# Scaling the next pair's keys behind the row-sum addition on GpSimd, and the first pair's loads split over two queues

## Chip, cores and metric

The kernel runs on one core of one Trainium2 chip. The metric is the device time of one execution in microseconds (us). Before the change it is 1041.75 us, the median of three runs (1041.70 to 1041.97). The profile discussed here is one profiled execution with a span of 1039.9 us, in which TensorE was granted 0.993 of its full clock.

## What is computed

Thresholded attention over 8 batches and 8 heads (sequence 576, head size 64), and then a mixture of experts in which a hash of the token number picks one of 8 experts:

```python
scores = scale * np.matmul(q, k.transpose(0, 1, 3, 2))
thresh = np.max(scores, axis=-1, keepdims=True) - tau
scores = np.where(scores >= thresh, scores, -1000000000.0)
scores = scores - np.max(scores, axis=-1, keepdims=True)
attn = np.exp(scores)
attn = attn / (np.sum(attn, axis=-1, keepdims=True) + 1e-09)
attn_out = np.matmul(attn, v)
# x = attn_out as (B*S, H*D)
expert_idx = token_ids * np.int64(2654435761) % np.int64(E)
for e in range(E):
    xe = x[expert_idx == e]
    out[expert_idx == e] = np.maximum(xe @ w1[e], 0.0) @ w2[e]
```

All data is float32. The host lays q and k out with the head size ahead of the sequence (`qT`, `kT`), which is done before the launch and is not part of the time.

## The kernel before, in words

**Two stages.** The attention takes the first 484 us or so, the experts the rest. The change lies in the attention stage and in its start.

**Pairs and steps.** Attention works on pairs: two heads of one batch, 32 pairs in all, numbered `p`. A pair is cut into five steps `s`. Step 0 holds the last 64 queries of both heads (128 rows), steps 1 to 4 hold 128 queries each, once for each head (`j` = 0, 1). So a pair has nine score tiles of 128 x 576. The main loop runs over `n = 5*p + s`, and the order of instructions in each engine's queue is the order in which the loop's body emits them (`tc.manual_schedule()`); the framework adds only the semaphore waits.

**One score tile.** TensorE makes the scores from `q_sb` and the scaled `k_sb` (`score`, L201), two 288-wide halves into two banks of PSUM. VectorE negates them into `ns` and takes their minimum (`negate`, L212). GpSimd adds the threshold constant to that minimum (`thr`, L219, a 128 x 2 operation). ScalarE takes the exponential (`expo`, L226) into `w`. One step later VectorE masks: `w = (ns <= thr) * w`, with the row sum as accumulator (`mask`, L237; it reads two tiles, `ns` and `w`, both in SBUF). TensorE then transposes `w` (`turn_w`, L248), ScalarE copies the transposes out (`put_wT`, L264 and L269), and TensorE multiplies by v (`av_part`, L279).

**Finishing a pair.** The last masks of pair `q` are emitted in step 0 of the next pair. In step 1 GpSimd adds 1e-9 to the nine row sums (`add_eps`, two tiny operations at L309); they wait for the last mask of pair `q`. In step 2 VectorE takes the reciprocal (L603), which waits for `add_eps`. In step 0 of the pair after that, VectorE multiplies the transposed output by it (`put_xm`, L318).

**Keys.** `load_pair(p + 2)` loads keys and queries two pairs ahead, at step 0, all on the SyncE queue. Keys come in three pieces (L163, L164, L165), queries in two of 288 KB (L167). `scale_k(p + 1)` (L181) multiplies the next pair's keys by 1/8 and by the `keep_any` flag, in place, in one GpSimd operation over 128 x 576. Before the change it is emitted at the top of step 1, so that GpSimd takes it ahead of that step's `add_eps`:

```python
if s == 1 and p + 1 < NP:
    scale_k(p + 1)
...
if s == 1 and 0 <= q < NP:
    add_eps(q)
```

**The routing of tokens.** In between, VectorE does the small integer work of the routing. It is a generator, `route()`, cut into pieces by bare `yield` lines. The loop takes one piece at step 3 (at its top) and one at step 0 (behind `negate`, ahead of `put_xm`). As the generator is cut before the change, nearly all heavier pieces (the 128 x 288 operations L366, L374, L408, L412, L415 and the like) fall into step 0 and the light ones into step 3; the piece at L381 to L388, which contains two small matmuls in between, falls into step 3. Once slots are known, 36 scatters on GpSimd (L464) are spread over pairs 12 to 20, four to a pair, none of them in step 1. Ten row gathers (L101) are emitted in pairs 26 and 27, one at each step.

**The start.** The first pair's queries are issued on the ScalarE queue, its keys on SyncE behind the 512-byte load of tau; then follow the token numbers, v and the second pair. GpSimd scales the whole first k tile, then writes its constants (iota, masks, memsets), then takes `thr` of step 0, and then `scale_k(1)`.

Of the kernel before, what the change touches and what calls it, by code (L numbers as in the profile page):

```python
# [14 lines left out]
ALU = mybir.AluOpType  # L15
# [5 lines left out]
def kernel(  # L21
# [12 lines left out]
    nc = tc.nc  # L34

    B, H, D, S = qT.shape
    N, DIN = out.shape
    E, _, F = w1.shape
    P = 128
    HP = H // 2  # L40
    NP = B * HP
# [3 lines left out]
    SCALE = 1.0 / float(D) ** 0.5  # L45
    assert D == 64 and S == 4 * P + 64 and SCALE == 0.125 and E == 8
    S2 = S // 2
    NQ = 4
    TAIL = NQ * P
# [38 lines left out]
    keep_any = consts.tile([P, 1], FP32, name="keep_any")  # L88
# [32 lines left out]
    with tc.tile_pool(name="a_q", bufs=1) as a_q, \  # L121
# [26 lines left out]
        av = ps_av.tile([P, 2, 512], FP32, name="av")  # L148
        kts, rss, recs, scs, nss, stats, ws = {}, {}, {}, {}, {}, {}, {}

        def load_pair(p, q_engine=nc.sync):
            hp, b = divmod(p, B)
            h0 = 2 * hp
            q_sb = q_bufs[p % 3]
            k_sb = a_k.tile([P, 2, S2], FP32, name="k_sb")
            kts[p] = k_sb


            def keys(c0, shift, width):
                ap = [[S, D], [D * S + shift, 2], [1, width]]  # L160
                return bass.AP(tensor=kT.tensor, offset=(b * H + h0) * D * S + c0, ap=ap)

            nc.sync.dma_start(out=k_sb[0:64, :, 64:S2], in_=keys(64, -64, S2 - 64))  # L163
            nc.sync.dma_start(out=k_sb[0:64, :, 0:64], in_=keys(0, TAIL, 64))  # L164
            nc.sync.dma_start(out=k_sb[64:P], in_=keys(S2, -64, S2))  # L165
            for r in range(2):
                q_engine.dma_start(out=q_sb[64 * r:64 * r + 64],  # L167
                                   in_=qT[b, h0:h0 + 2].rearrange("h d s -> d h s"))

        def load_v(p):  # L170
            hp, b = divmod(p, B)
# [8 lines left out]
        def scale_k(p):  # L180
            nc.gpsimd.tensor_scalar(out=kts[p][:], in0=kts[p][:], scalar1=keep_any[:],  # L181
                                    scalar2=SCALE, op0=ALU.mult, op1=ALU.mult)
# [121 lines left out]
        def add_eps(p):  # L304

            rec = a_st.tile([P, 2 * NS], FP32, name="rec")
            rs = rss.pop(p)
            for i, cols in ((0, 9), (9, 1)):
                nc.gpsimd.tensor_scalar(out=rec[:, i:i + cols], in0=rs[:, i - i // 9:i - i // 9 + cols],  # L309
                                        scalar1=1e-9, scalar2=None, op0=ALU.add)  # L310
            recs[p] = rec
# [20 lines left out]
        def route():  # L332
# [22 lines left out]
            nc.gpsimd.memset(keep[:, :, 0:1], 0.0)  # L355
            nc.gpsimd.memset(ones_e[:], 1.0)
            yield

            nc.vector.tensor_scalar(out=eid[:], in0=tid32[:, :, 0], scalar1=E - 1, scalar2=None,
                                    op0=ALU.bitwise_and)
# [4 lines left out]
                                    in0=eidf[:, None, :].to_broadcast([P, E, NTC]),  # L367
# [3 lines left out]
            for e in (0, E // 2):  # L371
# [6 lines left out]
                if e == 0:  # L378
# [14 lines left out]
                                    scalar2=float(P - 1), op0=ALU.add, op1=ALU.max)  # L393
            nc.vector.tensor_scalar(out=ot_i[:], in0=ot_i[:], scalar1=7, scalar2=None,
                                    op0=ALU.logical_shift_right)
# [4 lines left out]
                                         op1=ALU.add)  # L400
# [19 lines left out]
                                    scalar2=None, op0=ALU.bitwise_and)  # L420
            nc.vector.tensor_scalar(out=rank_i[:, 2], in0=rank_i[:, 0], scalar1=13, scalar2=None,
                                    op0=ALU.logical_shift_right)
# [5 lines left out]
                                    op0=ALU.mult)  # L428
            yield
            nc.vector.tensor_scalar(out=ovt[:], in0=ovt[:], scalar1=float(P),  # L430
                                    scalar2=float((E - 1) * CAP), op0=ALU.mult, op1=ALU.add)
# [8 lines left out]
                                           op0=ALU.add, op1=ALU.add)  # L440
# [6 lines left out]
                out=oc, in0=iota_f[:, 0:NOV, None].to_broadcast([P, NOV, E]),  # L447
# [6 lines left out]
                                    scalar1=float(E - 1), scalar2=None, op0=ALU.min)  # L454
# [6 lines left out]
        def scatters():  # L461
# [13 lines left out]
            for _ in range(4):  # L475
# [2 lines left out]

        nc.sync.dma_start(out=tau_in[:],
                          in_=bass.AP(tensor=tau.tensor, offset=0, ap=[[0, P], [1, 1]]))  # L480
        load_pair(0, nc.scalar)
        nc.sync.dma_start(out=tid32[:],
                          in_=bass.AP(tensor=dataclasses.replace(token_ids.tensor,
                                                                 shape=[2 * N], dtype=I32),
# [8 lines left out]
                                op0=ALU.is_ge)  # L493
# [8 lines left out]
            nc.vector.memset(v_sb[64:P, 4, 0:64], 0.0)  # L502
        nc.vector.memset(oT[:, 0:64], 0.0)
        nc.vector.memset(xg_bufs[0][:], 0.0)

        def constants():

# [64 lines left out]
        with tc.manual_schedule():  # L572

            tr = ps_tr.tile([P, 2, 512], FP32, name="tr")
            for _ in range(18):
                nc.tensor.transpose(tr[:, 0, 0:P], ident[:], ident[:])
            scale_k(0)
            constants()
            next(pieces)
            score(0, 0)  # L580
            for n in range(LAST + NS + 1):
                p, s = divmod(n, NS)
                m = n - 2
                if s == 0 and p + 2 < NP:
                    load_pair(p + 2)
                if s == 0 and p + 1 < NP:
                    load_v(p + 1)
                if s == 1 and p + 1 < NP:
                    scale_k(p + 1)
                if s == 2 and p in (20, 24):  # L590
                    load_w1(p // 4 - 5)
                if s == 2 and p in (22, 26):
                    load_w2((p - 22) // 4)

                if s == 3 and n < LAST:
                    next(pieces, None)
                if s == 1 and 3 <= p < 2 + len(xg_bufs):
                    nc.sync.dma_start(out=xg_bufs[p - 2][:], in_=xg_bufs[0][:])
                q = p - 1
                if s == 1 and 0 <= q < NP:  # L600
                    add_eps(q)
                if s == 2 and 0 <= q < NP:
                    nc.vector.reciprocal(recs[q][:], recs[q][:])  # L603
                if n == LAST:
                    tr = ps_sc.tile([P, 2, 512], FP32, name="sc")
                    early_xT(tr, 0, 2, 0, CO - 1)
                if s == 0 and p >= 2:
                    turn_o()
                if n == LAST:
                    tr = ps_sc.tile([P, 2, 512], FP32, name="sc")  # L610
                    early_xT(tr, 2, 4, 0, CO - 1)
                if s in (1, 2) and 0 <= q < NP and n != LAST + 1:
                    av_part(q, 0, ((0, 1, 2), (3, 4))[s - 1])
                if n < LAST and s in (1, 2):
                    negate(n, 0)
                    expo(n, 0)
                if s == 2 and 0 <= q < NP:
                    put_oT(0)
                if n > LAST:
                    fill(1)  # L620
                turned = 0 <= m < LAST
                if turned:
                    tr = turn_w(m, 0)
                    put_wT(m, 0, tr)
                if n == LAST:
                    tr = ps_sc.tile([P, 2, 512], FP32, name="sc")
                    early_xT(tr, 4, 5, 0, CO - 1)
                    put_xm(p - 2)
                    av_part(q, 0, (0, 1, 2))
                if n >= LAST:  # L630
                    fill(1)
                if s in (3, 4) and 0 <= q < NP:
                    av_part(q, 1, ((0, 1, 2), (3, 4))[s - 3])
                if n < LAST and s not in (1, 2):
                    negate(n, 0)
                    expo(n, 0)
                if s == 0 and n < LAST:
                    next(pieces, None)
                if s == 0 and p >= 2 and n != LAST:
                    put_xm(p - 2)  # L640
                if s == 4 and 0 <= q < NP:
                    put_oT(1)
                if s in (3, 4) and turned:
                    tr = turn_w(m, 1)
                if n + 1 < LAST:
                    score(n + 1, 0)
                if s == 4 and turned:
                    put_wT(m, 1, tr)
                if n < LAST and heads(n) == 2:
                    negate(n, 1)  # L650
                    expo(n, 1)
                if s == 3 and turned:
                    put_wT(m, 1, tr)
                if n + 1 < LAST:
                    score(n + 1, 1)
                if s in (0, 1) and turned:
                    tr = turn_w(m, 1)
                    put_wT(m, 1, tr)
                if 0 < n <= LAST:
                    for j in range(heads(n - 1)):  # L660
                        mask(n - 1, j)
                if s != 1 and placed:
                    next(scatter_pieces, None)


                g = n - G0
                if 0 <= g < 2 * KT:
                    fetch(g // KT, g % KT, 0)
                if n == LAST:
                    fill(1)  # L670
            for g in range(2 * KT):
                fetch(g // KT, g % KT, 1)
            fill(FO * 2 * (CO - 1) - 18)
            tr = ps_tr.tile([P, 2, 512], FP32, name="tr")
            early_xT(tr, 0, KT, CO - 1, CO)
            fill(18)
            late_h()
# [123 lines left out]
```

## Time and profile before

| stretch of the span, us | TensorE busy | VectorE busy | ScalarE busy | GpSimd busy |
|---|---|---|---|---|
| 0 to 11 | 5.54 | 2.71 | 1.28 | 3.09 |
| 11 to 26 | 12.66 | 14.58 | 11.49 | 5.77 |
| 180 to 310 | 127.92 | 128.82 | 111.94 | 87.90 |
| 456 to 484 | 26.55 | 15.76 | 14.27 | 4.20 |
| 484 to 1040 | 545.54 | 56.28 | 48.92 | 109.24 |

The table is the view of busy time by stretches. A busy time close to the length of its stretch says that the engine hardly ever stood still there. In the expert stage that is TensorE alone; in the attention TensorE and VectorE are both close to it. TensorE's ends are modelled, so a busy TensorE is not proof that it works at its peak. The share of VectorE over the whole span, 49%, is an average over the two stages and says nothing of either.

### The profile page before, as it was taken

To read this page: it belongs to the slowest core of one execution; us is meant where nothing else is said; L and a number is where in the kernel's file an instruction comes from. 1 tells how busy PE (TensorE), PEld (TensorE's weight loads), DVE (VectorE), ACT (ScalarE), POOL (GpSimd) and SP (SyncE) were. 2 spreads that over 40 slices of the span, in tenths; PEclk is the share of its full clock that TensorE was granted. 3 is DMA by queue.
4 is the path that set the end of the run, shared out by engine and by line. 5 is a ranking of instruction groups with operands and counts; after the bars stand their busy time and mean duration, and the time that the engine had idled before them with its cause. 6 is when DMAs were issued, how large, how long until landed. Compare 5 with 4: busy or idle time off the path is not lost. (4 is left out here: it accounts for less than half of the span.)

```text
span 1039.9 us, 19768 instructions
## 1 busy us (share of the span) xinstructions
PE 1017.7 (98%) x7432; PEld 613.6 (59%) x7432; DVE 514.3 (49%) x1352; ACT 445.8 (43%) x725; POOL 315.6 (30%) x431
## 2 busy tenths in 40 slices
PE   6999999999999999999999999999999999999996
PEld 4666666656666666666547557466475574664752
DVE  6999999999999999992300101001001010010000
ACT  4888888888898888891201000000010000000100
POOL 3233332667762246232514022140140221001001
PEclk8999999999999999999999999999999999999998
DMA  7355544445464869301404231242042312200000
GB/s 163 80 127 135 126 118 111 102 116 115 101 178 111 258 139 245 82 25 28 136 36 135 100 104 56 106 141 84 33 135 100 105 54 104 98 5 32 10 18 28
DMA packets 91732, 103.46 MB, mean 99 GB/s; under 512 B 24301, under 2 KB 65391, under 8 KB 91636
## 3 DMA queue, kind: packets, MB, share of 16 engines
q1 hardware_dynamic: 83156, 82.68, 29.6%
q0 software_dynamic: 8192, 18.91, 5.3%
q8 instruction: 60, 0.98, 0.4%
q10 hardware_dynamic: 288, 0.59, 0.2%
q14 instruction: 36, 0.29, 0.1%
HBM read 81.87 MB, written 20.01 MB: 98 GB/s over the span
## 5 line engine op out<-in xcount | busy, mean ns | idle before, releaser
L717 PE MATMUL o_ps<-w_sb,h 128*122 128x512 f32 x640 | 280.6, 592 | 0.0
L226 ACT ACTIVATE w<-ns,nmx 128x576 f32<-128x576 f32 x288 | 220.3, 776 | 48.5 <-DVE ns L212 48.5
L703 PE MATMUL sc<-xT,w_sb 128*128 128x305 f32 x896 | 231.2, 419 | 0.0
L237 DVE SCALAR_TENSOR_TENSOR w<-ns,thr,w 128x576 f32<-128x576 f32 x288 | 230.3, 831 | 0.0
L212 DVE TENSOR_SCALAR_CACHE_REDUCE ns<-sc 128x576 f32<-128x576 f32 x288 | 205.8, 746 | 10.1 <-PE sc L201 9.4
L703 PEld LDWEIGHTS sc<-xT,w_sb 128*128 128x128 f32 x896 | 169.1, 189 | 63.4 <-issue 3.4
L717 PEld LDWEIGHTS o_ps<-w_sb,h 128*122 128x122 f32 x640 | 115.5, 185 | 138.9 <-issue 138.5
L201 PE MATMUL sc<-k_sb,q 64*128 64x288 f32 (+1 forms) x1280 | 183.8, 430 | 6.2 <-DMA v<-in_v_dram 3.9
L721 POOL DMA_INDIRECT out_dram<-o,gidx x40 | 39.6, 989 | 414.0 <-ACT o L720 400.4
L219 POOL TENSOR_SCALAR thr<-nmx,drop 128x2 f32<-128x2 f32 (+1 forms) x160 | 98.8, 617 | 206.5 <-DVE ns L212 197.2
L248 PEld LDWEIGHTS tr<-ident,w 64*128 64x128 f32 x2624 | 106.8, 139 | 87.8 <-ACT wT_b L269 27.0
L711 DVE TENSOR_SCALAR h<-sc 128x610 f32<-128x610 f32 x28 | 22.2, 793 | 256.9 <-PE sc L703 256.9
L720 ACT COPY o<-o_ps 122x512 f32<-122x512 f32 x40 | 23.4, 586 | 293.4 <-PE o_ps L717 293.4
L248 PE MATMUL tr<-ident,w 64*128 64x64 f32 x2624 | 139.1, 230 | 2.5 <-ACT wT_a L269 2.0
L696 DVE COPY xT<-xT_ps 128x488 f32<-128x488 f32 x35 | 23.3, 665 | 183.4 <-PE xT_ps L694 183.4
L201 PEld LDWEIGHTS sc<-k_sb,q 64*128 64x128 f32 (+1 forms) x1280 | 93.1, 178 | 33.2 <-DVE ns L212 15.5
L279 PE MATMUL av<-wT_a,v 128*64 128x320 f32 (+1 forms) x704 | 100.4, 418 | 0.2 <-DVE xm L318 0.2
L709 ACT ACTIVATE h<-sc 128x610 f32<-128x610 f32 x28 | 19.0, 680 | 182.7 <-PE sc L703 182.7
L269 ACT COPY wT_a<-tr 128x512 f32<-128x512 f32 (+1 forms) x128 | 81.8, 639 | 20.2 <-PE tr L248 20.1
L269 ACT COPY wT_b<-tr 128x512 f32<-128x512 f32 (+1 forms) x128 | 81.2, 634 | 6.3 <-PE tr L248 3.8
L279 PE MATMUL av<-wT_b,v 128*64 128x256 f32 x640 | 83.2, 389 | 0.0
L279 PEld LDWEIGHTS av<-wT_a,v 128*64 128x64 f32 x704 | 43.7, 136 | 28.9 <-DVE xm L318 0.3
(97 smaller groups left out, 517.1 us busy)
## 6 DMA issues: line engine op xcount, KB each, us to landing
w_sb<-in_moe_w_dram SPq DMA_DIRECT2D x16, 2048.0 KB
q<-in_q_dram SPq DMA_DIRECT2D x62, 288.0 KB
v<-in_v_dram SPq DMA_DIRECT2D x32, 256.0 KB
xa_scratch<-xm SPq DMA_DIRECT2D x24, 256.0 KB
k_sb<-in_k_dram SPq DMA_DIRECT2D x32, 144.0 KB
k_sb<-in_k_dram SPq DMA_DIRECT2D x32, 112.0 KB
xg<-xg SPq DMA_DIRECT2D x9, 256.0 KB
xb_scratch<-xm SPq DMA_DIRECT2D x8, 256.0 KB
```

The costliest lines, as they stand in the source:

```text
L201: nc.tensor.matmul(sc[out_rows, i, 0:S2], lhsT=q_sb[rows, h, q0:q1], rhs=k_sb[rows, h], start=True, stop=True)
L212: nc.vector.tensor_scalar(out=ns[:].rearrange("p (i s) -> p i s", i=2), in0=sc[:, :, 0:S2], scalar1=-1.0, scalar2=None, op0=ALU.mult, op1= ...
L219: nc.gpsimd.tensor_scalar(out=thr[:, 0:j + 1], in0=stats[n][0][:, 0:j + 1], scalar1=drop[:], scalar2=None, op0=ALU.add)
L226: nc.scalar.activation(w, nss[n, j][:], AF.Exp, bias=stats[n][0][:, j:j + 1], scale=-1.0)
L237: nc.vector.scalar_tensor_tensor(out=w, in0=nss.pop((n, j))[:], scalar=stats[n][1][:, j:j + 1], in1=w, op0=ALU.is_le, op1=ALU.mult, accum_ ...
L248: nc.tensor.transpose(dst[:, r, 64 * c:64 * c + 64], src[rows, c0:c0 + P], ident[rows, rows])
L269: nc.scalar.copy(dst, tr[:, :, 0:64 * n_c].rearrange("p r (c q) -> p r c q", c=n_c))
L279: nc.tensor.matmul(av[64 * j:64 * j + 64, g, c0:c1], lhsT=v_sb[:, c, 64 * j:64 * j + 64], rhs=wT[g][:, i, c0:c1], start=(c == 0), stop=stop)
L703: nc.tensor.matmul(h_ps[:, i, 0:width], lhsT=w1_sb[:, co, fo * P:fo * P + P], rhs=xT[:, co, i * width:i * width + width], start=(co == 0), ...
L717: nc.tensor.matmul(o_ps[0:rows], lhsT=h_sb[:, fo, kt * rows:kt * rows + rows], rhs=w2_sb[:, fo, :], start=(fo == 0), stop=(fo == FO - 1))
L720: nc.scalar.copy(o_sb[0:rows], o_ps[0:rows])
L721: nc.gpsimd.indirect_dma_start(out=out[:, :], out_offset=bass.IndirectOffsetOnAxis(ap=idx, axis=0), in_=o_sb[:], in_offset=None, bounds_ch ...
```

## The change: what it does and what it is for

It has three parts.

1. `scale_k(p + 1)` is emitted behind `add_eps(q)` in step 1, not at the top of the step. On GpSimd the row-sum additions of the finished pair come first, and the scaling of the next pair's keys follows. It is meant to keep the long scaling from standing ahead of the additions, and from running beside the masks.
2. The first pair's loads are reordered: the third key piece goes to the ScalarE queue, at its head; behind it come the last 64 columns of the queries, which are all that step 0 needs. The other 512 columns follow on SyncE behind the other two key pieces. The first k tile is scaled by two engines, one head by VectorE and one by GpSimd, at once.
3. `route()` gets one more `yield` behind its memsets, so that each later piece comes half a turn later: what was taken at step 0 is now taken at step 3, and the other way round.

```diff
-        def load_pair(p, q_engine=nc.sync):
+        def load_pair(p):
...
+            def queries(engine, r, c0, c1):
+                engine.dma_start(out=q_sb[64 * r:64 * r + 64, :, c0:c1],
+                                 in_=qT[b, h0:h0 + 2, :, c0:c1].rearrange("h d s -> d h s"))
+
             nc.sync.dma_start(out=k_sb[0:64, :, 64:S2], in_=keys(64, -64, S2 - 64))
             nc.sync.dma_start(out=k_sb[0:64, :, 0:64], in_=keys(0, TAIL, 64))
-            nc.sync.dma_start(out=k_sb[64:P], in_=keys(S2, -64, S2))
+            (nc.sync if p else nc.scalar).dma_start(out=k_sb[64:P], in_=keys(S2, -64, S2))
+            if p:
+                for r in range(2):
+                    queries(nc.sync, r, 0, S)
+                return
+
             for r in range(2):
-                q_engine.dma_start(out=q_sb[64 * r:64 * r + 64],
-                                   in_=qT[b, h0:h0 + 2].rearrange("h d s -> d h s"))
+                queries(nc.scalar, r, TAIL, S)
+            for r in range(2):
+                queries(nc.sync, r, 0, TAIL)
...
             nc.gpsimd.memset(ones_e[:], 1.0)
             yield
+            yield
...
-        load_pair(0, nc.scalar)
+        load_pair(0)
...
+        for j, engine in enumerate((nc.vector, nc.gpsimd)):
+            engine.tensor_scalar(out=kts[0][:, j], in0=kts[0][:, j], scalar1=keep_any[:],
+                                 scalar2=SCALE, op0=ALU.mult, op1=ALU.mult)
...
-            scale_k(0)
             constants()
...
-                if s == 1 and p + 1 < NP:
-                    scale_k(p + 1)
...
                 if s == 1 and 0 <= q < NP:
                     add_eps(q)
+                if s == 1 and p + 1 < NP:
+                    scale_k(p + 1)
```

## The prediction, made before the changed kernel was run

> **What bounds the kernel.** I began with busy time by engine on the page and by stretch:
>
> ```profile
> PE 1017.7 (98%) x7432; PEld 613.6 (59%) x7432; DVE 514.3 (49%) x1352; ACT 445.8 (43%) x725; POOL 315.6 (30%) x431
> 26.00:180.00 154.00, 153.57 (x1868) 95.40 (x1868) 151.88 (x433) 131.96 (x216) 47.11 (x86) 1.00 0.47 116
> 310.00:456.00 146.00, 145.96 (x1786) 91.21 (x1782) 144.27 (x391) 125.90 (x206) 58.28 (x95) 1.00 0.61 154
> ```
>
> In the last two rows, the columns after the length are busy TensorE, its weight loads, VectorE, ScalarE, GpSimd. TensorE and VectorE both fill the attention. TensorE's ends are modelled, so the timeline must say which one waits. In an ordinary pair (VectorE and GpSimd lines only; start, duration):
>
> ```profile
> 423.33 0.82 DVE L318 TENSOR_TENSOR xm<-av,rec 128x640 f32<-128x640 f32 x1
> 423.58 0.30 POOL L219 TENSOR_SCALAR thr<-nmx,drop 128x1 f32<-128x1 f32 x1 [1.50 <-DVE ns L212]
> 423.85 0.75 POOL L181 TENSOR_SCALAR k_sb<-k_sb,keep_any 128x576 f32<-128x576 f32 x1
> 424.06 1.14 DVE L237 SCALAR_TENSOR_TENSOR w<-ns,thr,w 128x576 f32<-128x576 f32 x1
> ...
> 426.04 0.54 POOL L309 TENSOR_SCALAR rec<-rs 128x9 f32<-128x9 f32 x2 [1.44 <-DVE w L237]
> 426.55 0.08 DVE L212 DVE_READ_ACCUMULATOR ns<-sc 128x1 f32 x1
> 426.55 0.75 DVE L212 TENSOR_SCALAR_CACHE_REDUCE ns<-sc 128x576 f32<-128x576 f32 x1
> ...
> 427.23 0.81 DVE L237 SCALAR_TENSOR_TENSOR w<-ns,thr,w 128x576 f32<-128x576 f32 x1
> 427.48 0.73 POOL L219 TENSOR_SCALAR thr<-nmx,drop 128x2 f32<-128x2 f32 x1 [0.90 <-DVE ns L212]
> ```
>
> VectorE runs back to back, so it sets the pace, with one hole a pair: `negate` at 419.75 idles 0.19 us for the scores, 6.01 us after the reciprocal. The mask at 424.06 takes 1.14 us where others take 0.81. The scaling beside it ends at 424.60, the mask 0.60 us later, at 425.20. So the mask waited for GpSimd, then streamed for 0.60; undisturbed it has used 0.81 - 0.60 = 0.21 before streaming.
>
> Across VectorE's timeline 16 masks exceed 0.835 us, each ending 0.59 to 0.61 us after a scaling. Their excess over 0.812 adds up to **6.0 us**; the group row (831 ns mean, x288) agrees roughly: 0.019 x 288 = 5.5. The largest three, 0.8 us each, are of this kind:
>
> ```profile
> 196.19 1.03 POOL L464 DMA_INDIRECT slot_scratch<-tok,slot_i  x1 [0.39 <-issue]
> 197.02 1.61 DVE L237 SCALAR_TENSOR_TENSOR w<-ns,thr,w 128x576 f32<-128x576 f32 x1
> 197.26 0.76 POOL L181 TENSOR_SCALAR k_sb<-k_sb,keep_any 128x576 f32<-128x576 f32 x1
> ```
>
> Where a scatter comes ahead of the scaling at another moment, the scaling falls beside two `negate`s, which stay at 0.75, and the reciprocal waits for the additions instead:
>
> ```profile
> 242.83 0.76 POOL L181 TENSOR_SCALAR k_sb<-k_sb,keep_any 128x576 f32<-128x576 f32 x1
> 243.67 1.11 POOL L309 TENSOR_SCALAR rec<-rs 128x9 f32<-128x9 f32 x2
> 244.82 0.22 DVE L603 RECIPROCAL rec<-rec 128x10 f32<-128x10 f32 x1
> ```
>
> From one reciprocal to the next this pair takes 13.90 us (244.82 to 258.72), the ordinary one 14.23 (413.74 to 427.97), the last pair, which has no next keys to scale, 13.89. Its hole is 0.19 again; in the pair whose reciprocal waits, it is gone. So **13.89 us is the floor**, and 0.19 us of VectorE delay between the last mask and the hole is free.
>
> [...] mask (two SBUF inputs) 1.14, `negate` (reads PSUM) 0.75, and `thr` takes 0.73 at 427.48 where it meets a mask, 0.30 at 423.58. [...] Here TensorE idles 3.93 us before the first scores, and the granted clock from 9 to 14 us is 0.50.
>
> **Part 1, the order on GpSimd.** No operation is added. Additions start 1.93 us ahead of the reciprocal, as now (they wait for the mask, not the scaling), and end at -1.39. The scaling follows, an estimated 0.06 us of dispatch (0.04 from 197.22 to 197.26, 0.08 ahead of 243.67), 0.75 of work: -1.33 to -0.58. Beside it run the two `negate`s. The next mask starts at -0.74 and streams from -0.53: margin 0.05, and 0.19 of delay is free. `thr` becomes ready at -0.49, behind the scaling. It isn't delayed, and its masks come only after the reciprocal and two `negate`s. The keys aren't urgent: those scaled at 110.22 are first read at 122.45. So all 6.0 us go. Where the reciprocal waits today, 0.19 us comes back as the hole: net 0. **-6.0 us.**
>
> **Part 3, the pieces.** A piece at step 0 costs its whole interval, since VectorE has no slack there: a 128x288 piece 0.37 (109.62 to 109.99), and that pair's 14.30 = 13.89 + 0.37 + 0.03 of excess. At step 3 it precedes the hole and costs what exceeds 0.19: today's light ones (0.09) leave the hole's end at +6.01. Today step 0 carries 0.37, 0.37, 0.36, 0.41, 0.41, 0.38, 0.37, 0.58, 0.18, 0.17, 0.43, 0.11, 0.33, 0.33, 0.39 = 5.2, and step 3 costs 0.6 (the piece with two matmuls, which holds TensorE too). After: the long ones less 0.19 each, none below 0, give 2.45; the light ones 0.6 in step 0; the first two token operations, hidden now, 0.2. The matmul piece grows: in step 0 its matmuls wait for ScalarE to empty the transpose tile. In the pair at 109.62 that copy ends at 110.26, so the piece would cost about 1.05, not 0.6. 5.8 - 4.3 = **-1.5 us.**
>
> **Part 2, the start.**
>
> ```profile
> 8.42 0.75 POOL L181 TENSOR_SCALAR k_sb<-k_sb,keep_any 128x576 f32<-128x576 f32 x1 [6.94 <-DMA k_sb<-in_k_dram]
> 10.61 0.76 DVE L212 TENSOR_SCALAR_CACHE_REDUCE ns<-sc 128x576 f32<-128x576 f32 x1 [5.96 <-PE sc L201]
> 11.77 0.74 POOL L181 TENSOR_SCALAR k_sb<-k_sb,keep_any 128x576 f32<-128x576 f32 x1
> 15.71 0.81 DVE L237 SCALAR_TENSOR_TENSOR w<-ns,thr,w 128x576 f32<-128x576 f32 x1
> ```
>
> Everything waits for keys until 8.42. By the DMA view the ScalarE queue (576 KB of queries) fills most engines until 6.2, and only after that do the keys flow. After: keys and query tails, 288 + 64 KB, come first. At 152 to 309 GB/s (bins from 3 to 5 us) that is 1.2 to 2.4 us from 2.4 on[...]: 5.4 (4.9 to 6.2). Scaling half a tile on VectorE has no row: between 0.3 (half of 0.6 streaming) and 0.45 (its 128x288 tensor operations); on GpSimd 0.4 (half of 0.75) to 0.75. The two may exclude each other, so no gain from halving: 0.75 together. First scores 6.3, [...] first `negate` near 7.2 instead of 10.61. The 512 KB of remaining queries land near 8, so step 1's `negate` comes at 8.5 instead of 11.87.
>
> Not all of it survives. GpSimd's queue is `thr` of step 0, `scale_k(1)`, `thr` of step 1; the first mask of step 1 (15.71 now) waits for the last. The second pair's keys are issued behind two query loads moved to this queue, about 0.7 us later than now: 9.05 instead of 8.35 for the last piece. With 3 us to landing (tau: issued 0.91, used 4.11) GpSimd gets them at 12.0, scales until 12.8, `thr` until 13.1, and the mask starts at 13.2. **-2.5 us**; 3.8 if this wait doesn't bite, about 0 if the keys land late.
>
> **The sum.** 6.0 + 1.5 + 2.5 = 10.0; 1041.75 - 10.0 = **1031.8 us**. The expert stage keeps it: TensorE is busy 545.54 of its 556 us and merely starts earlier. Loads have room there (DMA share 0.22).
>
> **Rivals.**
> - **`thr` gets the pair ahead of the waiting mask.** In the scatter and gather pairs (about 12) additions start only after the scatter (242.78), so the scaling ends about 0.1 after the mask wants to stream, with `thr` ready. If GpSimd keeps the pair, 0.1 + 0.3 - 0.19 = 0.2 a pair, 2.4. With the scaling 0.1 later than I take it, the other 18 lose 0.16 each: 2.9. For: at 197.26 GpSimd took it while the mask was due. Against: nobody had waited yet. 1031.8 + 5.3 = 1037.1. 17%.
> - **The start gains nothing**, its loads only changing places: 1034.3. For: data of the same size must arrive before step 1. 13%.
> - **The start gains 3.8**: 1030.5. 10%.
> - **The pieces and part 1 are given back to the scores** (TensorE 153.57 of 154 busy): only the start, 1039.3. Against: the 13.89 pairs. 5%.
> - **Slower.** The scaling starts about 0.5 us late, in front of the mask, each of 31 masks waits 0.6, 0.41 beyond the hole: +12.7, 1044.5. Against: nothing stands between additions and scaling. 3%.
>
> My forecast has 52%. Range 1029.8 to 1037.2: the start's ends below, the `thr` case above. Faster by over 0.2% (below 1039.7): 0.95; within: 0.02; slower: 0.03.
>
> **What would show it.** Masks all near 0.81 and no group mean of 831; pairs at 13.89 to 13.90 after 310 us; the scaling between additions and `thr`, ending ahead of the mask's streaming; the reciprocal never idle; pieces leaving +6.01 to +6.2 at the hole; one pair near 15.1 around the matmul piece; first `negate` near 7.2. I am wrong if masks at -0.74 stretch, or `thr` waits make VectorE idle beyond the first pair.

## The result and the profile after

The changed kernel takes 1032.05 us (median of four runs, 1031.32 to 1032.89), the kernel before 1041.86 beside it: ratio 0.9905, 95% interval 0.9888 to 0.9922. The profiled execution has a span of 1030.0 us (before 1039.9). In the changed kernel the line numbers of the loop lie 10 to 13 higher: `score` L211, `negate` L222, `thr` L229, `mask` L247, `add_eps` L319, `put_xm` L328, reciprocal L616, `scale_k` L191, and L517 is the scaling of the first tile.

Busy time by engine, two stretches as before (the second one shifted by the 10 us that the attention got shorter), and the group of masks (count, busy us, mean ns, idle):

```profile
PE 1012.2 (98%) x7432; PEld 613.0 (60%) x7432; DVE 507.8 (49%) x1353; ACT 445.7 (43%) x725; POOL 316.2 (31%) x431
26.00:180.00 154.00, 153.10 (x1907) 96.36 (x1904) 152.68 (x438) 133.62 (x219) 46.72 (x87) 1.00 0.48 119
300.00:446.00 146.00, 146.00 (x1830) 92.36 (x1826) 144.57 (x401) 128.74 (x211) 62.91 (x98) 1.00 0.61 156
L247 DVE SCALAR_TENSOR_TENSOR w<-ns,thr,w 128x576 f32<-128x576 f32 x288 | 226.0, 817 | 0.0
```

The columns are those of the prediction. Both engines are as full as before; the same instructions simply fit into less time. The mean mask fell from 831 to 817 ns. Eleven masks still exceed 0.835 us (16 before), by 1.5 us in all (6.0 before).

An ordinary pair, lines from VectorE's and GpSimd's timelines, one after the other (start, duration; the accumulator reads are left out):

```profile
402.15 0.75 DVE L222 TENSOR_SCALAR_CACHE_REDUCE ns<-sc 128x576 f32<-128x576 f32 x1
402.83 0.75 DVE L222 TENSOR_SCALAR_CACHE_REDUCE ns<-sc 128x576 f32<-128x576 f32 x1
403.50 0.81 DVE L247 SCALAR_TENSOR_TENSOR w<-ns,thr,w 128x576 f32<-128x576 f32 x1
404.24 0.21 DVE L616 RECIPROCAL rec<-rec 128x10 f32<-128x10 f32 x1
...
402.32 0.54 POOL L319 TENSOR_SCALAR rec<-rs 128x9 f32<-128x9 f32 x2 [1.77 <-DVE w L247]
402.95 0.75 POOL L191 TENSOR_SCALAR k_sb<-k_sb,keep_any 128x576 f32<-128x576 f32 x1
403.76 0.73 POOL L229 TENSOR_SCALAR thr<-nmx,drop 128x2 f32<-128x2 f32 x1
```

The scaling lies beside the two `negate`s, from -1.29 to -0.54 us of the reciprocal, and the mask at -0.74 keeps its 0.81. Now `thr` is what meets the mask, at 0.73. Nobody waits for it there. From here on "pair 30" stands for the time from the reciprocal of pair 30 to the next one; there are 32 reciprocals, of pairs 0 to 31, so the intervals are pairs 0 to 30. Of pairs 15 to 29, ten take 13.90 or 13.91 us, and none is over 14.15.

A pair with a scatter ahead of the additions, in the same two views:

```profile
194.41 0.94 DVE L247 SCALAR_TENSOR_TENSOR w<-ns,thr,w 128x576 f32<-128x576 f32 x1
195.28 0.20 DVE L616 RECIPROCAL rec<-rec 128x10 f32<-128x10 f32 x1
...
191.82 1.47 POOL L475 DMA_INDIRECT slot_scratch<-tok,slot_i  x1 [0.39 <-issue]
193.37 0.54 POOL L319 TENSOR_SCALAR rec<-rs 128x9 f32<-128x9 f32 x2
194.00 0.75 POOL L191 TENSOR_SCALAR k_sb<-k_sb,keep_any 128x576 f32<-128x576 f32 x1
194.73 0.78 POOL L229 TENSOR_SCALAR thr<-nmx,drop 128x2 f32<-128x2 f32 x1
```

Here the additions, held up by the scatter, start 1.04 us ahead of the mask instead of 1.18, and the scaling ends at 194.75, after the mask would have begun to stream (194.62, an estimate: its start and the 0.21 us by which 0.81 exceeds 0.60). The mask ends at 195.35, 0.60 after the scaling. So the mask, which had waited, went first, and `thr`, queued right behind the scaling, took 0.78 and ended 0.16 after the mask. The mask loses 0.13 us.

The start (VectorE and GpSimd):

```profile
6.04 0.37 DVE L517 TENSOR_SCALAR k_sb<-k_sb,keep_any 128x288 f32<-128x288 f32 x1 [1.75 <-DMA k_sb<-in_k_dram]
7.58 0.76 DVE L222 TENSOR_SCALAR_CACHE_REDUCE ns<-sc 128x576 f32<-128x576 f32 x1 [1.18 <-PE sc L211]
12.44 0.81 DVE L247 SCALAR_TENSOR_TENSOR w<-ns,thr,w 128x576 f32<-128x576 f32 x1
25.65 0.76 DVE L222 TENSOR_SCALAR_CACHE_REDUCE ns<-sc 128x576 f32<-128x576 f32 x1 [1.29 <-PE sc L211]
...
6.10 0.68 POOL L517 TENSOR_SCALAR k_sb<-k_sb,keep_any 128x288 f32<-128x288 f32 x1 [4.54 <-DMA k_sb<-in_k_dram]
10.83 0.94 POOL L191 TENSOR_SCALAR k_sb<-k_sb,keep_any 128x576 f32<-128x576 f32 x1 [2.07 <-DMA k_sb<-in_k_dram]
```

The first mask of step 1 comes at 12.44 instead of 15.71, 3.27 us earlier, the first reciprocal at 24.15 instead of 27.98. In that lead of 3.83 us lie also a mask that took 1.29 us before and takes 0.81 now, and a routing piece of 0.37 us that now comes behind the reciprocal. TensorE's granted clock from 9 to 14 us is 1.00 (0.50 before); ahead of the first scores TensorE idles 0.75 us (3.93 before). But then VectorE stands still for 1.29 us at 24.36, for the scores, which it did not do before. By the second reciprocal (39.78 instead of 42.23) only 2.45 us are left. From there to the last but one reciprocal the kernel takes 406.18 us, before 413.86: 7.68 less. Pair 30 gives 0.28 us back (12.28 us, before 12.00), and from the last reciprocal to the end nothing changes (571.76, before 571.81).

### The profile page after: what moved, and what is told of

Same layout as the page of the kernel before. It is cut to its first block, busy times and chain, and to the rows that moved or that the text cites. A ratio compares the mean times of both kernels' runs of the same rounds, so it can differ in the third digit from the quotient of the medians.

```text
span 1030.0 us, 19768 instructions
## 1 busy us (share of the span) xinstructions
PE 1012.2 (98%) x7432; PEld 613.0 (60%) x7432; DVE 507.8 (49%) x1353; ACT 445.7 (43%) x725; POOL 316.2 (31%) x431
## 5 line engine op out<-in xcount | busy, mean ns | idle before, releaser
L247 DVE SCALAR_TENSOR_TENSOR w<-ns,thr,w 128x576 f32<-128x576 f32 x288 | 226.0, 817 | 0.0
L222 DVE TENSOR_SCALAR_CACHE_REDUCE ns<-sc 128x576 f32<-128x576 f32 x288 | 205.4, 746 | 5.9 <-PE sc L211 5.2
L211 PE MATMUL sc<-k_sb,q 64*128 64x288 f32 (+1 forms) x1280 | 179.0, 423 | 1.3 <-DVE k_sb L517 0.7
L229 POOL TENSOR_SCALAR thr<-nmx,drop 128x2 f32<-128x2 f32 (+1 forms) x160 | 102.3, 639 | 188.5 <-DVE ns L222 176.5
L211 PEld LDWEIGHTS sc<-k_sb,q 64*128 64x128 f32 (+1 forms) x1280 | 93.4, 178 | 23.1 <-DVE ns L222 9.3
L279 ACT COPY wT_a<-tr 128x512 f32<-128x512 f32 (+1 forms) x128 | 81.7, 638 | 20.1 <-PE tr L258 19.6
```

What stands on the lines that cost most here:

```text
L211: nc.tensor.matmul(sc[out_rows, i, 0:S2], lhsT=q_sb[rows, h, q0:q1], rhs=k_sb[rows, h], start=True, stop=True)
L222: nc.vector.tensor_scalar(out=ns[:].rearrange("p (i s) -> p i s", i=2), in0=sc[:, :, 0:S2], scalar1=-1.0, scalar2=None, op0=ALU.mult, op1= ...
L229: nc.gpsimd.tensor_scalar(out=thr[:, 0:j + 1], in0=stats[n][0][:, 0:j + 1], scalar1=drop[:], scalar2=None, op0=ALU.add)
L247: nc.vector.scalar_tensor_tensor(out=w, in0=nss.pop((n, j))[:], scalar=stats[n][1][:, j:j + 1], in1=w, op0=ALU.is_le, op1=ALU.mult, accum_ ...
L279: nc.scalar.copy(dst, tr[:, :, 0:64 * n_c].rearrange("p r (c q) -> p r c q", c=n_c))
```

## The experiments

The first four ran on one chip, on which the kernel before takes what it takes above (1041.94 us and 1041.86). The others ran on three further chips, on which the kernel before takes 1054 to 1059 us; across chips, ratios and stretches of the trace are compared, not times. The times in the expectations are meant for the first chip. "The stretch" below is the time from the second to the last but one reciprocal.

### Part 1 alone

```diff
-                if s == 1 and p + 1 < NP:
-                    scale_k(p + 1)
...
                     add_eps(q)
+                if s == 1 and p + 1 < NP:
+                    scale_k(p + 1)
```

> The kernel before with the scaling of the keys emitted behind the row-sum additions, and nothing else. Theory [...]: the 6.0 us of stretched masks go, all masks are near 0.81 us in the ordinary pairs, in the pairs with a scatter ahead of the scaling they are near 0.93 (as in the changed kernel) and that hides in the hole ahead of the fifth negate; nothing at the start changes. So 6.0 us less than before, 1035.8. Rival 1 (the time is given back to TensorE's scores): at most 1 us, about 1041. Rival 2 (the gain of the whole change comes from the start and the pieces, and the order on GpSimd is worth only the three 0.8 us pairs): 2.4 us, 1039.4.

Measured: 1035.97 us (1035.66 to 1036.28), ratio 0.994 (0.9924 to 0.9957); before on the same chip 1041.94 (median of 23). That is 5.97 us, from one moved line, as the theory had it. Eight masks are still long, by 1.35 us in all. The three pairs of 14.85, 15.04 and 15.03 us, whose masks stood behind a scatter and the scaling, take 13.95, 14.23 and 14.30.

### Part 2 alone

The hunks of the diff for `load_pair`, the two-engine scaling and the removed `scale_k(0)`, with no other.

> The kernel before with the first pair's loads reordered and its k scaled by two engines, and nothing else. Theory A: the first mask of step 1 starts 3.3 us earlier than before (15.71 to about 12.4), then TensorE's clock falls to half for some 3 us at about 19 to 22 us because TensorE is too idle there, and VectorE stands still for about 1.4 us; net 2 to 2.5 us less than before, 1039.3 to 1039.8. Theory B (the stall after the first reciprocal comes from something else in the changed kernel, the new place of the scaling or of the pieces): no stall, 3.3 to 3.8 us less, 1038.0 to 1038.5.

Measured: 1040.28 us (1039.07 to 1041.46, twenty runs), ratio 0.9983 (0.9977 to 0.9990): 1.7 us. Neither theory came true: the granted clock stays at 1.00 up to 26 us and VectorE has no long wait behind the first reciprocal, and yet the gain is smaller than either said. At the second reciprocal it is 3.04 us ahead of before, so more reaches that point than the end (2.0 in the spans). Pairs 1 and 5 then take 0.24 and 0.29 us more than before (14.50 and 14.59), pair 30 takes 0.28 more (12.28), and pair 19 takes 0.22 more (14.40), where one mask takes 1.48 us instead of 1.27.

In pairs 1, 5 and 30 ScalarE stands still ahead of a copy without a cause that the profile shows (it names ScalarE's own operation before), and 3 to 5 us later VectorE waits for scores longer than its usual 0.19 us. Two of the three, ScalarE's line and then VectorE's:

```profile
43.14 0.59 ACT L279 COPY wT_a<-tr 128x512 f32<-128x512 f32 x1 [0.28 <-ACT w L236]
48.35 0.76 DVE L222 TENSOR_SCALAR_CACHE_REDUCE ns<-sc 128x576 f32<-128x576 f32 x1 [0.23 <-PE sc L211]
...
456.36 0.69 ACT L274 COPY wT_a<-tr 128x640 f32<-128x640 f32 x1 [0.29 <-ACT oT L305]
460.06 0.76 DVE L222 TENSOR_SCALAR_CACHE_REDUCE ns<-sc 128x576 f32<-128x576 f32 x1 [0.47 <-PE sc L211]
```

All ten traces with part 2 have these three pauses, of 0.26 to 0.29 us, ahead of the same copies; the four traces without part 2 have none there. So most of what part 2 loses later comes back in every run. Part 2 gives ScalarE's queue three loads instead of two; whether the pauses come from that is open.

### Parts 1 and 2, without the extra yield

The changed kernel, less this line:

```diff
             yield
-            yield
```

> The changed kernel without the extra yield, so that the longer routing pieces are back in step 0. Theory A (the hole ahead of the fifth negate takes 0.27 us of a piece, as the trace of the changed kernel shows): the pieces cost about 3.1 us more, 1035.1. Theory B (it takes 0.19 us, as the prediction had it): 1.5 us more, 1033.5. In both the pair with the two small matmuls in step 3 is shorter than in the changed kernel (14.9 instead of 15.0), and those with a 0.37 us piece are 14.25 to 14.3 instead of 13.98 to 14.15.

Measured: 1034.07 us (1033.33 to 1034.67), ratio 0.992 (0.9903 to 0.9936). Parts 1 and 2 add up: 5.97 + 1.66 = 7.63 alone, 7.87 together. What is left for part 3 is 1034.07 - 1032.05 = 2.0 us, between the 3.1 of theory A and the 1.5 of theory B; as each median is of four runs that spread over 1.3 to 1.6 us, it excludes neither. In the traces, pairs 2 to 14, which hold most of the routing, take 185.86 us here and 183.42 in the changed kernel: 2.4 us, and 2.8 with pair 1, which holds a piece too.

### TensorE kept busy in the start

The changed kernel, with transposes whose results are not used:

```diff
+                if 2 <= n <= 5:
+                    for _ in range(3):
+                        nc.tensor.transpose(av[:, 0, 0:P], ident[:], ident[:])
```

> The changed kernel with three more transposes of the identity into an unused bank at the end of steps n = 2 to 5 (twelve in all, about 0.2 us each), which compute nothing that is used. Theory A (the clock of TensorE fell because it was too idle between 14 and 19 us): the granted clock stays 1.00 from 10 to 26 us, the scores before the second negate after the first reciprocal come in time, VectorE's 1.3 us of waiting there goes, and the time is 1.0 to 1.4 us below the changed kernel, 1030.6 to 1031.0. Theory B (the scores are late for their own dependencies): no gain, or 0.3 us more for the added work.

Measured: 1031.42 us (1030.65 to 1032.33), ratio 0.9894 (0.9878 to 0.9911). The clock stays at 1.00 up to 26 us, and the idle of VectorE behind the first reciprocal is 0.65 us instead of 1.29. The gain of 0.6 lies within the ranges of the two, so it isn't shown. Nor does the trace show one in the start: the second reciprocal comes at 40.40, behind the 39.78 of the changed kernel's trace, in which the clock fell.

### The scaling later still

The changed kernel, with two memsets of 128x288 between the additions and the scaling.

```diff
+                if s == 1 and 0 <= q < NP and p + 1 < NP:
+                    for _ in range(2):
+                        nc.gpsimd.memset(h_0[:, 0, 0:288], 0.0)
                 if s == 1 and p + 1 < NP:
                     scale_k(p + 1)
```

> The changed kernel with two memsets of an idle 128x288 tile on GpSimd (about 0.34 us each) between the row-sum additions and the scaling, in every pair, so that the scaling starts about 0.7 us later and is still running when the next mask wants to stream. Theory (the moment of the scaling is what counts[...]): the masks ahead of the reciprocal take about 1.4 us instead of 0.81, the thresholds behind them wait for the mask, the hole of 0.27 us takes a part of it, 0.35 to 0.63 us a pair are lost over 29 pairs, 1044 to 1047. Rival 1 (the threshold addition, ready behind the scaling, goes first): 0.3 us a pair more, 1053 to 1056. Rival 2 (GpSimd's moment doesn't matter, only that the additions come first): 1032 to 1033.

Measured: 1045.77 us (1044.55 to 1046.97), ratio 0.9902 (0.9884 to 0.9921), the changed kernel's own. So the theory, which meant 12 to 15 us more than the changed kernel, failed; that the time lies in its range comes from the slower chip. VectorE and GpSimd around a reciprocal, and below them the groups of masks and scalings:

```profile
82.01 0.81 DVE L247 SCALAR_TENSOR_TENSOR w<-ns,thr,w 128x576 f32<-128x576 f32 x1
82.75 0.21 DVE L619 RECIPROCAL rec<-rec 128x10 f32<-128x10 f32 x1
...
81.42 0.73 POOL L615 MEMSET h<- 128x288 f32 x2
82.13 1.31 POOL L191 TENSOR_SCALAR k_sb<-k_sb,keep_any 128x576 f32<-128x576 f32 x1
...
L247 DVE SCALAR_TENSOR_TENSOR w<-ns,thr,w 128x576 f32<-128x576 f32 x288 | 224.5, 812 | 0.0
L191 POOL TENSOR_SCALAR k_sb<-k_sb,keep_any 128x576 f32<-128x576 f32 x31 | 39.6, 1279 | 2.1 <-DMA k_sb<-in_k_dram 2.1
```

The delay of 0.7 us puts the scaling 0.12 us behind the start of the mask, and now the scaling is the one that waits: 1.31 us, 1.28 on average (0.75 beside the `negate`s). No mask is long, and pairs 2 to 10 take the times of the changed kernel within 0.02 us each. So the place directly behind the additions isn't needed; what cost time was a scaling that starts ahead of a mask and ends after the mask, by the estimate of 0.21 us into its time, would have begun to stream. A scaling that starts between the two places wasn't tried.

### The scaling replaced, in its old place

The kernel before, in which from the third pair on two memsets stand in place of the scaling. The scaling is left out, so the scores of these pairs are unscaled and the output is not that of the task; only the time is of use.

```diff
         def scale_k(p):
-            nc.gpsimd.tensor_scalar(out=kts[p][:], in0=kts[p][:], scalar1=keep_any[:],
-                                    scalar2=SCALE, op0=ALU.mult, op1=ALU.mult)
+            if p < 2:
+                nc.gpsimd.tensor_scalar(out=kts[p][:], in0=kts[p][:], scalar1=keep_any[:],
+                                        scalar2=SCALE, op0=ALU.mult, op1=ALU.mult)
+                return
+            for _ in range(2):
+                nc.gpsimd.memset(h_0[:, 0, 0:288], 0.0)
```

> The kernel before, in which from the third pair on the scaling of the keys is left out and two memsets of an idle 128x288 tile (about 0.67 us together, GpSimd writes and reads nothing) stand in its old place. Theory [...]: no mask above 0.84 us from the third pair on, 5.5 to 6 us less than before, 1036. Rival [...]: masks stretched as before by up to 0.3 us, 1040 to 1041.5.

Measured: 1049.63 us (1048.43 to 1051.76), ratio 0.9936 (0.9915 to 0.9957), 6.3 us less than the kernel before on that chip. No mask is long (mean 812 ns), although 0.74 us of GpSimd work stand in the old place. GpSimd's line and VectorE's in the pair that the prediction showed:

```profile
421.82 0.74 POOL L186 MEMSET h<- 128x288 f32 x2
422.07 0.81 DVE L241 SCALAR_TENSOR_TENSOR w<-ns,thr,w 128x576 f32<-128x576 f32 x1
```

The memsets start 0.25 us ahead of the mask, the scaling started 0.21 ahead of it; the mask took 1.14 us beside the scaling and takes 0.81 beside the memsets. The ratio is that of part 1 alone, 0.994: moving the scaling gains what leaving it out gains. So no cost of the scaling to VectorE is seen beside the long masks. The rival, in which memsets stretch the masks too, is refuted; what it is in the scaling that does it, the run doesn't show.

### The pieces moved to step 3, and with TensorE kept busy

The changed kernel's `yield`s are moved, and the call at step 0 is dropped (only this part of the edit is shown), so that all routing pieces run at step 3; the second kernel adds the transposes above for n = 2 to 4.

```diff
-                if s == 0 and n < LAST:
-                    next(pieces, None)
```

> The changed kernel with the routing cut anew: no piece at step 0, and light operations grouped so that each piece at step 3 takes about 0.3 us (15 pieces to the slot numbers, which come two pairs later). Theory (the hole ahead of the fifth negate swallows 0.27 us of a piece at step 3, a piece at step 0 costs all of it): the light pieces' 0.6 us at step 0 go and the piece with the two matmuls costs 0.35 instead of 1.09; 1.0 to 1.3 us less than the changed kernel, 1030.8 to 1031.1. Rival (what is left of the pieces doesn't matter, the pairs are bound by TensorE): 1032.

> As pieces_in_step3, with three more transposes of the identity into an unused bank at the end of steps n = 2 to 4 (nine in all), not in step 5, where in clock_filled they stood ahead of the attention product. Theory A (the stall behind the first reciprocal is TensorE's low clock): the clock stays 1.00 from 10 to 26 us, the stall falls from 1.3 us to 0.3 or less, another 0.6 to 1.0 us, 1029.9 to 1030.4. Theory B (the low clock comes and goes from run to run whatever stands in these steps): as pieces_in_step3.

Measured: 1045.47 us (1044.07 to 1046.50), ratio 0.9892 (0.9874 to 0.9910); and 1044.5 (1043.45 to 1045.11), ratio 0.9884 (0.9868 to 0.9900). Both looked a little better than the changed kernel, so the same three kernels were run on one chip (the second expectation speaks of four pieces, but the kernel moves all of them):

> The changed kernel once more, beside the two below on one chip. Both theories: first negate near 7.6 us, first mask of step 1 near 12.5, pairs mostly 13.90 to 14.00. Theory A (the stall after the first reciprocal comes from TensorE's clock, which falls in its idle time of 15 to 20 us): the clock is below 0.6 for some 3 us of that stretch and VectorE idles 0.7 to 1.4 us at 25 to 26 us in pair 0. Theory B (a chance of one run): the clock is full there in this run and pair 0 takes near 14.3.

> The changed kernel with its first four routing pieces in step 3 of the pair instead of step 0. Theory A (a piece at step 3 costs less: the two-instruction int pieces 0.28 instead of 0.41, the matmul piece no 1.1 us wait): 1.0 to 1.5 us below the changed kernel on the same chip, all of it in pairs 2 to 12. Theory B (the chance differences of the later pairs drown it): within 0.7 us of it.

> As the one before, with three small transposes that keep TensorE busy in 15 to 23 us. Theory A: clock full until 26 us, pair 0 below 14.6, and 0.7 to 1.2 us below the one before, so 1.7 to 2.7 below the changed kernel on the same chip. Theory B (the filled clock gives nothing on the whole): within 0.5 of the one before.

Measured, in that order: 1046.42 us (1044.80 to 1046.91), ratio 0.9895 (0.9879 to 0.9912); 1047.5 (1045.1 to 1048.07), ratio 0.9911 (0.9894 to 0.9927); 1045.5 (1044.41 to 1045.77), ratio 0.9888 (0.9871 to 0.9904). The intervals overlap: neither is shown to beat the changed kernel, and the gains of 1.0 us and more that theory A had expected are not borne out. In the changed kernel's second trace the clock is full and pair 0 takes 14.49 us, as theory B had it.

In the traces step 3 alone takes 1.76 us less in pairs 2 to 12 (154.17 against 155.94), the matmul piece's wait among it. About 0.8 of it is in pairs 11 and 12, where the changed kernel now takes 14.22 and 14.41 us (14.03 and 14.01 in its first trace). Pairs 13 to 26 take 1.09 us more (198.87 against 197.78). Part of this is work put off: with one piece a pair the routing ends in pair 16, not 14, and the scatters run to pair 22, not 20. Both traces have eight waits of VectorE, of 0.22 to 0.53 us, in these pairs, beside the usual 0.19: some for scores, some ahead of `put_xm`, for which the profile names no releaser. What decides these waits stays open.

### The kernel before on a slower chip

> The kernel before, unchanged, with a profile on the chip of the last seven runs, to see what its longer time consists of. Theory A: the expert stage is longer (about 595 us from the last reciprocal to the end instead of 584, as in the other runs there) and the pairs after the twelfth take 0.1 to 0.4 us more here and there, while masks over 0.835 us are 16 as before and cost about 6 us; then the time from the second to the last reciprocal is 415 to 417 us, and the scaling put late (410.0) gains 5 to 7. Theory B: the pairs are as they were (413.9 from the second to the last reciprocal), and the scaling put late gains under 4 in that stretch.

Measured: 1056.88 us, a single run; it ran on yet another chip, which is slower in the same way. The last but one reciprocal lies 595.7 us ahead of the end (583.8 in the first trace), with the clock at 0.94 from 484 to 600 us. Two more pairs take 15.04 us, and 16 masks are long by 6.8 us in all. The stretch is 417.16 us, against 411.32 with the scaling left out, 410.03 with the scaling late and 409.59 in the changed kernel: gains of 5.8, 7.1 and 7.6, of which the last two hold part 3 as well. Leaving the scaling out, or putting it behind the mask's start, is worth about what was put down to the long masks (6.0 us in the first trace, 6.8 here).

The expectation took this chip for that of the runs before it; it isn't, so these differences hold only as far as the three chips are alike. Within one chip the ratios above say the same.

## Why the prediction was right, point by point

The sum held: 10.0 us forecast, 9.7 to 9.9 measured (medians of the kernel before 1041.75 and 1041.86, span 9.9). Its terms did so less evenly, and that they add up so well is in part luck.

- **Part 1, -6.0: right in size and cause.** 5.97 alone. The scaling starts 0.04 us later than taken (0.09 of dispatch instead of 0.06, from 402.86 to 402.95), which leaves the margin at 0.01 us, and still the ordinary masks stay at 0.81. So thin a margin was not needed: in the scatter pairs it is missed, and the hole takes the loss.
- **The rival in which `thr` goes ahead of the waiting mask is refuted.** ("The pair" that it gets or keeps in the prediction is whatever the mask waits for; the traces show the waiting, not what is held.) In the nine scatter pairs and two gather pairs the scaling ends late, as that rival had it, but each mask ends 0.59 to 0.61 us after it, and `thr` only 0.16 to 0.18 after the mask. The loss of 0.11 to 0.24 falls into the hole that comes later.
- **The slower rival did not come; its size was not tried.** The scaling follows the additions by 0.09 us. One that comes 0.67 us later lands behind the mask's start and waits itself; one that comes 0.5 later would still start ahead of it. Which of the two waits went in the main by which started first: mask 0.84 to 1.29 us where the scaling started first, scaling 1.28 on average where the mask did. Three masks of the kernel before are an exception: they started 0.19 to 0.25 us ahead of the scaling, at the end of a scatter (197.02 in the prediction), and still ended 0.6 after it, with 1.55 to 1.62 us. So did the mask of 1.48 us with part 2 alone, which started 0.13 ahead of the scaling, as far as in the kernel with the scaling late, where the scaling waited. What differs is what GpSimd was at when the mask began: a scatter or a `thr` in these four, a memset there. It is as if GpSimd had gone on from one operation to the next without letting the mask in; that is inferred, no run tests it.
- **Part 3, -1.5: right cause, probably too small; 2.0 by the medians, 2.4 to 2.8 in the traces.** The term that failed is the 0.19 us of free delay. In the changed kernel the hole of an ordinary pair, and the same place in the pair whose piece is the 128x36 reduction:

```profile
409.98 0.08 DVE L247 DVE_READ_ACCUMULATOR w<-ns,thr,w 128x1 f32 x1
410.26 0.76 DVE L222 TENSOR_SCALAR_CACHE_REDUCE ns<-sc 128x576 f32<-128x576 f32 x1 [0.19 <-PE sc L211]
...
127.92 0.07 DVE L247 DVE_READ_ACCUMULATOR w<-ns,thr,w 128x1 f32 x1
127.92 0.68 DVE L426 TENSOR_REDUCE rank_f<-incl 128x36 f32<-128x288 f32 x1
128.51 0.76 DVE L222 TENSOR_SCALAR_CACHE_REDUCE ns<-sc 128x576 f32<-128x576 f32 x1
```

The idle column counts from the end of the accumulator's read, but VectorE otherwise starts its next operation together with that read, as it starts the reduction here. From start to start the hole is 410.26 - 409.98 = 0.28 us. The reduction's interval is 0.59 us, and the fifth `negate` behind it, at the end of the next group, comes 6.33 us after the reciprocal instead of 6.01: 0.32 is charged, 0.27 hidden. The lines for this were in the trace before: 419.48 to 419.75 is 0.27. Besides, the two-instruction integer pieces take 0.28 at step 3, where 0.41 was carried over from step 0. With 0.27 and 0.28 in it the prediction's own sum gives an estimate of 2.7, which the traces bear out and the medians leave open.
- **The matmul piece: right.** 1.09 us from `row` to `put_xm` (63.53 to 64.62), forecast 1.05; VectorE idles 0.74 of it. The pair takes 15.01, forecast near 15.1.
- **Part 2, -2.5: the number held, the step did not.** The step said that GpSimd gets the second pair's keys at 12.0 and that the first mask of step 1 waits for `thr` until 13.2. They are taken at 10.83 (the 5.4 us for the first pair's keys rested on the author's estimate of the landing; they are taken at 6.04), `thr` follows at 11.74, the mask comes at 12.44, and VectorE doesn't wait. So the start itself gained 3.0 to 3.3 us, between the forecast and the rival's 3.8, and part of it was lost later, at ScalarE's pauses for the most part, which neither had. At the second reciprocal the lead over before is 2.45 us in the changed kernel's first trace, 2.83 in its second (against the kernel before on the slower chip), 3.04 with part 2 alone, 2.68 with parts 1 and 2. By the end, part 2 alone is worth 1.7.

So two misses of about half a microsecond to a microsecond, part 3 too small and part 2 too large by its worth at the end, cancelled. That is luck.

The low clock goes with a longer pair 0. The changed kernel's first trace in stretches of 1 us, with the granted clock third from the end,

```profile
19.00:20.00 1.00, 0.86 (x16) 0.44 (x10) 1.00 (x5) 1.00 (x2) 0.38 (x1) 0.78 0.62 150
20.00:21.00 1.00, 1.00 (x10) 0.78 (x8) 1.00 (x3) 0.90 (x3) 0.18 (x1) 0.50 0.69 168
21.00:22.00 1.00, 1.00 (x6) 0.57 (x4) 1.00 (x3) 0.55 (x1) 0.55 (x1) 0.50 0.98 251
22.00:23.00 1.00, 1.00 (x14) 0.81 (x12) 1.00 (x5) 0.15 (x1) 0.62 (x3) 0.52 1.05 241
23.00:24.00 1.00, 1.00 (x10) 0.48 (x10) 1.00 (x3) 1.00 (x2) 0.94 (x2) 1.00 1.14 205
```

and the same of its second:

```profile
20.00:21.00 1.00, 0.86 (x18) 0.53 (x12) 1.00 (x5) 1.00 (x3) 0.30 (x1) 1.00 0.58 149
21.00:22.00 1.00, 0.86 (x8) 0.35 (x8) 1.00 (x3) 0.97 (x3) 0.27 (x1) 1.00 0.42 53
```

In the first trace the clock is halved, VectorE then idles 1.29 us for the scores, and pair 0 takes 15.63 us. At full clock the same kernel's pair 0 takes 14.49. The kernel with pieces in step 3 shows both as well: 15.70 with the low clock at 21 to 24 us, 14.49 where it fell at 9 to 12 us instead. But the lead at the second reciprocal hardly differs: the second trace reached the first reciprocal 0.92 us later than the first (25.07 and 24.15), and the second one 0.22 earlier (39.56 and 39.78). And with the transposes, at full clock, pair 0 still takes 14.97. How much of the lead the low clock costs is not shown.

## What to carry to other kernels

Where a long GpSimd operation meets a two-input operation of VectorE, don't ask only whether they overlap, but which starts first. Here the mask took 0.84 to 1.29 us where the scaling started first, and the scaling 1.28 on average where the mask did (straight behind a scatter or a `thr`, though, masks that had started first took 1.48 to 1.62). Look in the trace for operations of VectorE that keep their time beside it, as `negate` does here with 0.75 us, and put it there, or late enough to be the one that waits. Read slack between two operations from start to start, since the idle column may leave out what normally overlaps (0.19 against 0.28 us here). And don't take a gain in the first microseconds for a gain at the end: of 3.0 us at the second reciprocal 2.0 were left.

## What the runs showed of the hardware

- **ScalarE pauses at fixed places, and an edit of the start moves them.** Three pauses of 0.26 to 0.29 us stand in all ten traces with part 2. The four without it have one pause, of 0.28 to 0.35 us, at 281 to 285 us.
- **The low clock moves from run to run.** The low stretch lasts about 3.4 us in the changed kernel's first trace (an estimate from the bins above: 0.44 us of the bin at 0.78, two whole bins, 0.96 of the bin at 0.52) and begins near 19.6 us there, near 18.5 with the scaling late, near 20.9 in the first run with pieces in step 3 (by the same count as long in these two); in the changed kernel's second trace there is none up to 26 us. In the kernel before, the low clock from 9 to 14 us follows an idle of 3.93 us; no such idle comes ahead of it here: TensorE's longest idle from 13 to 19.6 us is 0.68 us, at 16 to 18 us it is busy 0.93 of 2.00. Part 2 alone, with 0.87 of 2.00, kept its full clock. It was full in all three traces with extra transposes, which speaks for idle time as the cause; of the seven traces with part 2 and without transposes, four kept it full from 15 to 26 us too, so three don't prove it.
- **Halving the first scaling gains little.** Beside VectorE's half (0.37 us) GpSimd's half takes 0.68 instead of half of 0.75, and 0.68 or 0.69 in all ten traces with part 2: as if the two excluded each other, which was one of the prediction's two bounds.
- **The first scores differ in speed at a recorded full clock.** From 6 to 10 us the score matmuls take 414 ns in the median in the changed kernel's first trace and 684 in its second, and the first `negate` starts at 7.58 and 8.00. Why isn't known.
